# A fused attention and two-layer kernel: the attention's norms and layer one's low parts move from GpSimd to VectorE, with a new set of due times

## The chip, the cores and the metric

The kernel runs on one core of a Trainium2 chip. Its engines are TensorE (PE, with PEld for the loading of weights), VectorE (DVE), ScalarE (ACT), GpSimd (POOL) and SyncE (SP), which issues the DMAs here. The metric is the device time of one execution in microseconds (us). The kernel before takes 846.47 us, the median of three runs (845.16, 846.47, 847.29).

## The reference

An attention with local masks (a window of 32 rows in four heads, a dilated one in the other four) feeds two layers with weights. q, k and v are float32; the weight matrices arrive as float64 words and are decoded to float32 on the chip.

```python
scores = np.where(masks, q @ k.T / 8, -1e9)       # 4 batches, 8 heads, 576 rows, 64 wide
attn = exp(scores - max) / (sum + 1e-9)
x = (attn @ v)                                    # 2304 tokens x 512
h = ((x @ w1) * (x @ w2)) @ w3                    # 512 -> 1024 -> 1024
x = h @ w_out                                     # 1024 -> 512
h = x @ w_in                                      # 512 -> 2048
g = (a0 + a1*h + a2*h**2 + a3*h**3) / (1 + |b0|*|h| + |b1|*h**2 + 1e-6)
out = g @ w_out2                                  # 2048 -> 512
```

## The kernel before

Tokens stand along the free dimension, in five chunks of 480 (one of 384). Each value that enters a large matmul is kept as a high part (rounded to the matmul's format) and a low part (value minus high part), so that a product is made of three matmuls (`SPLIT`, L103).

The **first phase** (`phase1`, L589) does four things. It multiplies w3 by w_out once (`w3_mm`, L493), in plain float32, into eight tiles that are split into high and low (L504, L509). It runs the attention in 32 groups G of two heads and three row tiles of 96 (`att_qk` L375, `att_mask` L391, `att_exp` L408, `att_sums` L414, `att_norm` L420, `att_pt` L426, `att_pc` L433, `att_pv` L439). `att_high` and `att_low` (L480, L487) write x as high and low part into xs. For each chunk k, layer one (`l1`, L513) makes eight pairs of products of 12 matmuls each in the two banks `ab`; ScalarE copies the first (`l1_copy`), VectorE multiplies it with the second straight from its bank (`l1_mul`, L531), ScalarE casts the high part (`l1_high`, L536) and GpSimd subtracts for the low part (`l1_low`, L540). Layer two (`l2`, L543) follows in eight jobs of 12; its results leave their banks through ScalarE (L564) and VectorE (`x2l`, L569) and go to a DRAM tensor x2d. The fifth chunk's layer two is done in the second phase.

Weights arrive as 64-bit words in slabs of 512 KB (`load`, L243) and are decoded by a chain on ScalarE and VectorE: scale L257, shift L261, sign L265, low bits L280. With `by_act` a slab takes another route: ScalarE does one pass more (`top_bits`, L287) and VectorE only two (`ends` L292, `middle` L296). `BY_ACT3` is how many of the 24 slabs of w3 and w_out go by it. The slabs of w1 and w2 are split after that (L302, L306). The 32 slabs of the second phase's weights (moe2) are decoded one after the other through one slot, `w32`, and stored to a DRAM tensor wd (L310); the first four come back in `b_load` (L580) after the last of these stores.

**What sets the order.** Nothing of the first phase is in program order by hand. `Plan` (L114) holds each instruction group as a job with an engine, an estimated duration, what it follows, the buffers it takes and a due time. `dues` hands due times back along the dependences (`lead` shifts one; LEADS does so slab by slab), and `order` (L170) runs through time and gives each free engine the ready job that is due first. A job flagged `port`, and every POOL job, waits for the others so flagged. `tail` is the time from a job's end until another engine may start on it. The list sorted by start is what is issued, and each engine then works in that order, waiting in its queue. T (L613 to L617) holds nominal times of the main matmuls, with layer one and two stretched by PACE. The attention's due times hang on T, AHEAD, GAP and EARLY (L633 to L635), LEAD holds a group's start back, and B_FROM is where the due times of the moe2 stores begin (L809).

The **second phase** (`phase2`, L876) is a loop over 72 steps in program order: 12 matmuls (L906), the rational function on all of ScalarE, VectorE and GpSimd (L915 to L943), and 12 matmuls into the output (L956).

Of the kernel before, what the change touches and what calls it, by code (L numbers as in the profile page):

```python
# [10 lines left out]
F32 = mybir.dt.float32  # L11
# [4 lines left out]
ALU = mybir.AluOpType  # L16
# [10 lines left out]
CH = ((0, 480), (480, 480), (960, 384), (1344, 480), (1824, 480))  # L27
# [30 lines left out]
W3BANKS = (("acc", "ab"), ("acc", "ab"))  # L58


GAP0, GAP = 2.48, 9.89
LEAD = 83.96
AHEAD0, AHEAD = 10.57, 8.37
W3_AT = 8
PACE = 1.26

LEADS = (10.3, 12.3, 18.7, 24.0, 19.9, 5.3, 1.1, 21.6, 0.5, 9.0, -2.5, 3.0, -2.0, 35.8, -4.5, 15.1, -0.6, 1.0, -0.2, 3.4, -16.8, 2.7, -14.5, -8.7, -29.3, -24.1, -5.4, -5.8, -18.0, 1.2, -6.5, -5.3, -14.2, -16.4, -13.0, 2.4, -9.4, -18.5, -46.9, 13.0)
EARLY = (0.0, 0.6, 0.6, 0.5, 0.4, -2.9, -8.7, -2.1, 2.0, 3.3, -5.4, 10.3, -24.2, 19.9, 18.0, 2.9, 30.7, 24.0, 19.9, 23.2, 9.7, 2.9, -23.6, -53.8, -24.5, -67.9, -60.2, -3.4, -20.3, 1.3, 30.3, 41.5)
BY_ACT3 = 12
BY_ACT1, BY_ACT2 = 0, 16  # L70
B_FROM = 103.59


L2BANKS = (("acc", "ab"), ("acc", "sc"))
# [39 lines left out]
class Plan:  # L114
# [10 lines left out]
    def add(self, eng, work, fn, *args, after=(), new=(), use=(), due=None, port=False, tail=None,  # L125
            since=0.0, lead=0.0):


        if tail is None:
            tail = {"SP": 2.0, "PE": 0.2}.get(eng, 0.1)  # L130
        j = Job(len(self.jobs), eng, work, fn, args, [x for x in after if x is not None], new, due,
                port or eng == "POOL", tail, since, lead)
        for b in list(new) + list(use):
            b["users"].append(j)
        self.jobs.append(j)
        return j
# [83 lines left out]
class Kern:  # L220
# [199 lines left out]
    def att_norm(self, G, h):  # L420
        pr, sm = self.pr[G], self.sm[G]
        i = slice(3 * h, 3 * h + 3)
        self.nc.gpsimd.tensor_tensor(out=pr[:, i], in0=pr[:, i], op=ALU.mult,  # L423
                                     in1=sm[:, 2, i].unsqueeze(2).to_broadcast([QT, 3, P]))

    def att_pt(self, G, h):  # L426
# [110 lines left out]

    def l1_low(self, k, m):
        nt, w = CH[k][1], self.p2[k, m]
        self.nc.gpsimd.tensor_tensor(out=w[:, 1, 0:nt], in0=self.pp[k, m], in1=w[:, 0, 0:nt].bitcast(F32),  # L540
                                     op=ALU.subtract)

    def l2(self, k, h, i):  # L543
# [45 lines left out]
    def phase1(self):  # L589
# [20 lines left out]
        def act(k):  # L610
            return 0.08 + 0.00085 * CH[k][1]
# [9 lines left out]
        for ops in att_runs(2 * B * HP):  # L621
# [35 lines left out]
            for G, sc in qs:  # L657
                prb, smb, pTb = buf("pr"), buf("sm"), buf("pT")
                m0 = add("DVE", 0.64, self.att_mask, G, 0, after=[run], new=[prb, smb], use=sc[0:1])
                m1 = add("DVE", 0.64, self.att_mask, G, 1, after=[run, m0], use=[prb, smb, sc[1]])  # L660
                masked[G] = m1
                es = [add("ACT", 1.17, self.att_exp, G, h, after=[m], use=[prb, smb]) for h, m in enumerate((m0, m1))]
                su = add("DVE", 0.31, self.att_sums, G, after=es, use=[smb])
                no = [add("POOL", 0.79, self.att_norm, G, h, after=[su], use=[prb, smb]) for h in range(2)]
                pcs = []
                for h in range(2):
                    pb = buf(t_bank(G))
                    pt = add("PE", 0.25, self.att_pt, G, h, after=[no[h], done.get(G - 2)], new=[pb], use=[prb])
                    pts.setdefault(G, []).append(pt)
                    pcs.append(add("ACT", 0.31, self.att_pc, G, h, after=[pt] + pcs,  # L670
                                   new=[pTb] if h == 0 else [], use=[pb] + ([pTb] if h else [])))
                out[G] = pTb, pcs
# [88 lines left out]
        def l1_jobs(k, m):  # L761
            tb = [buf("t"), buf("t")]
            mm = []
            ready = [low[G] for b in range(B) if k in self.chunks(b) for G in range(b * 2 * HP, (b + 1) * 2 * HP)]
            for e in range(2):
                ab = buf("ab")
                mm.append((add("PE", mm12(k), self.l1, k, m, e, new=[ab], use=[xsb[k], w12b[2 * m + e]],
                               after=ready + [w12[2 * m + e]] + l1s[-1:], due=T["l1", k, m, e]), ab))
                l1s.append(mm[-1][0])
            d = T["l1", k, m, 1]  # L770
            c = add("ACT", act(k), self.l1_copy, k, m, after=[mm[0][0]], new=tb[0:1], use=[mm[0][1]], due=d)
            mu = add("DVE", act(k) + 0.09, self.l1_mul, k, m, after=[c, mm[1][0]], new=tb[1:2],
                     use=[tb[0], mm[1][1]], due=d + 2)
            pl, gbs = parts.setdefault(k, ([], []))
            gbs.append(buf("g"))
            hi = add("ACT", act(k) + 0.02, self.l1_high, k, m, after=[mu], new=gbs[-1:], use=[tb[1]], due=d + 5)
            pl.append(add("POOL", 0.08 + 0.0024 * CH[k][1], self.l1_low, k, m, after=[hi], use=[tb[1], gbs[-1]]))

        def l2_jobs(k):
            pl, gbs = parts[k]  # L780
# [346 lines left out]
```

## Time and profile before

| | us |
|---|---|
| median of three runs | 846.47 (845.16 to 847.29) |
| profiled execution | 844.74 |
| its span, first to last instruction | 842.9 |
| TensorE busy | 828.5 (98%) |
| VectorE busy | 581.2 (69%) |
| ScalarE busy | 539.4 (64%) |
| GpSimd busy | 330.5 (39%) |
| first matmul of the second phase (L906) | at 420.14 |

The profile is one execution, taken by the hardware profiler. Busy times are the union of an engine's instructions; a share over the whole span mixes two phases with different limits, so it is read by stages. "Idle before" is how long an engine stood before an instruction, and the releaser is the instruction that ended it. Starts are counted from the first instruction. L numbers are lines of the kernel.

### The profile page before, as it was taken

Reading aid. Unit: us, or ns where it says so; the run is one execution under the profiler, and the core shown is the slowest. Engines: PE = TensorE matmul, PEld = TensorE weight load, DVE = VectorE, ACT = ScalarE, POOL = GpSimd, SP = SyncE. Lnnn points to the kernel's source line nnn. Section 1 sums busy time; section 2 is a strip of 40 time slices with the busy share of each in tenths; the row PEclk is TensorE's granted clock in tenths of the full one; section 3 lists DMA queues with packets and bytes.
Section 4 is the critical chain, followed back from the end, with each engine's and each line's share of the span. In section 5 each row is a group of like instructions: output and inputs, shape, how many; then the busy total and the mean of one; then the engine's idle time right before and its main releaser. Section 6 shows DMA issues by size and latency. Waiting matters only on the chain.

```text
span 842.9 us, 12610 instructions
## 1 busy us (share of the span) xinstructions
PE 828.5 (98%) x4392; PEld 679.7 (81%) x4392; DVE 581.2 (69%) x1220; ACT 539.4 (64%) x1198; POOL 330.5 (39%) x289
## 2 busy tenths in 40 slices
PE   9999999999999989999999999999999999999998
PEld 6455788888889988888888788888888888888886
DVE  6899898555556644333327888788778777787775
ACT  6699885466456623312328877777777777786773
POOL 1123334133312411201215665565556556574442
PEclk9999999999999999999999999999999999999999
DMA  8988323554454234394151000010001000001112
GB/s 314 323 301 326 123 86 123 203 175 136 131 205 160 88 119 143 113 335 146 26 181 51 13 25 13 26 28 22 14 14 38 25 13 13 14 26 50 51 43 82
DMA packets 38271, 90.99 MB, mean 108 GB/s; under 512 B 4160, under 2 KB 9280, under 8 KB 38208
## 3 DMA queue, kind: packets, MB, share of 16 engines
q1 hardware_dynamic: 38208, 90.20, 31.7%
q8 instruction: 34, 0.56, 0.3%
q14 instruction: 29, 0.24, 0.1%
HBM read 69.60 MB, written 20.58 MB: 107 GB/s over the span
## 4 chain that ended last, share of the span: by engine, by line
PE 78%; DVE 8%; ACT 6%; DMA 5%; issue 2%; POOL 1%; SPq 0%; DVEq 0%; ACTq 0%; POOLq 0%
PE ab L519 21%; PE acc L956 11%; PE sc L956 11%; PE ab L906 10%; PE px L906 10%; PE acc L554 5%; DMA words<-moe_w 3%; PE sc L554 2%; PE ab L554 2%; ACT pr L411 2%; PE acc L445 1%; DMA words<-moe_w_out 1%; DVE dec L261 1%; PE sc L383 1%; DVE dec L265 1%
## 5 line engine op out<-in xcount | busy, mean ns | idle before, releaser
L519 PE MATMUL ab<-xs,w 128*128 128x480 f32 (+1 forms) x960 | 208.6, 374 | 4.1 <-DVE p L531 2.1
L519 PEld LDWEIGHTS ab<-xs,w 128*128 128x128 f32 x960 | 175.5, 188 | 28.8 <-DVE x2l L569 2.7
L917 POOL TENSOR_TENSOR y<-y,v 128x512 f32<-128x512 f32 x72 | 95.8, 1330 | 142.3 <-ACT y L916 142.1
L423 POOL TENSOR_TENSOR pr<-pr,sm 96x384 f32<-96x384 f32 x64 | 56.6, 907 | 170.9 <-DVE sm L418 98.0
L956 PE MATMUL acc<-w,gg 128*128 128x512 f32 x432 | 109.7, 391 | 1.5 <-ACT r L927 1.5
L956 PE MATMUL sc<-w,gg 128*128 128x512 f32 x432 | 109.3, 390 | 0.0
L540 POOL TENSOR_TENSOR pp<-p,pp 128x480 fp32r<-128x480 f32 (+1 forms) x40 | 50.1, 1256 | 141.9 <-ACT pp L536 141.9
L906 PE MATMUL ab<-XS,w 128*128 128x512 f32 (+1 forms) x480 | 105.4, 370 | 0.0
L906 PE MATMUL px<-XS,w 128*128 128x512 f32 (+1 forms) x480 | 105.3, 370 | 0.0
L943 POOL TENSOR_TENSOR gg<-t,gg 128x512 fp32r<-128x512 f32 x72 | 93.7, 1301 | 10.4 <-ACT gg L942 9.8
L906 PEld LDWEIGHTS px<-XS,w 128*128 128x128 f32 x480 | 83.8, 188 | 16.4
L906 PEld LDWEIGHTS ab<-XS,w 128*128 128x128 f32 x480 | 83.8, 188 | 16.4
L956 PEld LDWEIGHTS acc<-w,gg 128*128 128x128 f32 x432 | 80.7, 188 | 19.3 <-ACT r L927 1.9
L956 PEld LDWEIGHTS sc<-w,gg 128*128 128x128 f32 x432 | 80.8, 188 | 17.3
L411 ACT ACTIVATE pr<-pr,sm 96x128 f32<-96x128 f32 x192 | 74.4, 392 | 6.3 <-DVE sm L403 6.2
L257 ACT ACTIVATE dec<-words 128x512 f32<-128x512 f32 x72 | 48.0, 673 | 45.6 <-DMA words<-moe_w_in 21.3
L934 DVE SCALAR_TENSOR_TENSOR v<-y,cs,r 128x512 f32<-128x512 f32 x72 | 71.3, 991 | 0.0
L261 DVE TENSOR_SCALAR dec<-dec 128x512 int32<-128x512 int32 x44 | 28.8, 655 | 59.9 <-ACT dec L257 59.9
L926 ACT ACTIVATE r<-y,cs 128x512 f32<-128x512 f32 x72 | 52.3, 726 | 14.3 <-POOL y L917 14.1
L916 ACT ACTIVATE y<-v,cs 128x512 f32<-128x512 f32 x72 | 58.9, 817 | 2.5
L536 ACT CAST pp<-p 128x480 fp32r<-128x480 f32 (+1 forms) x40 | 23.1, 576 | 49.4 <-DVE p L531 49.3
L942 ACT CAST gg<-t 128x512 fp32r<-128x512 f32 x72 | 44.2, 614 | 14.2 <-DVE t L936 13.6
(96 smaller groups left out, 1295.1 us busy)
## 6 DMA issues: line engine op xcount, KB each, us to landing
words<-moe_w SPq DMA_DIRECT2D x32, 512.0 KB, 5.8
words<-moe_w_out SPq DMA_DIRECT2D x24, 512.0 KB, 4.4
words<-moe_w_in SPq DMA_DIRECT2D x16, 512.0 KB, 3.6
wd<-dec SPq DMA_DIRECT2D x32, 256.0 KB, 2.2
c<-wd SPq DMA_DIRECT2D x32, 256.0 KB, 2.7
vb<-v SPq DMA_DIRECT2D x16, 384.0 KB, 4.3
XS<-x2d SPq DMA_DIRECT2D x6, 1024.0 KB, 7.2
kT<-k SPq DMA_DIRECT2D x16, 304.0 KB, 4.2
```

The costliest lines, as they stand in the source:

```text
L411: self.nc.scalar.activation(out=pr[:, i], in_=pr[:, i], func=AF.Exp, scale=-1.0, bias=sm[:, 0, i:i + 1], accum_out=sm[:, 1, i:i + 1])
L423: self.nc.gpsimd.tensor_tensor(out=pr[:, i], in0=pr[:, i], op=ALU.mult, in1=sm[:, 2, i].unsqueeze(2).to_broadcast([QT, 3, P]))
L519: self.nc.tensor.matmul(t[:, 0:nt], w[:, s[0], c * P:(c + 1) * P], xs[:, s[1], c], start=n == 0, stop=n == 11)
L540: self.nc.gpsimd.tensor_tensor(out=w[:, 1, 0:nt], in0=self.pp[k, m], in1=w[:, 0, 0:nt].bitcast(F32), op=ALU.subtract)
L554: self.nc.tensor.matmul(self.l2_acc[k, n][:, 0:nt], self.W3o[m][0][:, a, n * P:(n + 1) * P], self.p2[k, m][:, c, 0:nt], start=m == 0 and ( ...
L906: nc.tensor.matmul(t[:, e * nt:(e + 1) * nt], w[:, s[0], c * P:(c + 1) * P], XS[blk][:, s[1], c], start=n == 0, stop=n == 11)
L916: nc.scalar.activation(out=w, in_=v, func=AF.Identity, scale=self.b1, bias=self.b0)
L917: nc.gpsimd.tensor_tensor(out=w, in0=w, in1=v, op=ALU.mult)
L926: nc.scalar.activation(out=r, in_=yy[i][1], func=AF.Ln, bias=self.c1)
L934: nc.vector.scalar_tensor_tensor(out=v, in0=w, scalar=self.c1, in1=r, op0=ALU.add, op1=ALU.mult)
L943: nc.gpsimd.tensor_tensor(out=t[:, 1], in0=u, in1=t[:, 0].bitcast(F32), op=ALU.subtract)
L956: nc.tensor.matmul(acc[g, blk][tk], t[:, s[0], j:j + P], w[:, s[1]], start=f + e == 0 and s == (0, 0), stop=f + e == FG - 1 and s == (1, 0))
```

## The change

Two functions issue on VectorE instead of GpSimd, `att_norm` (64 calls) and `l1_low` (40 calls), and their jobs in the plan move to VectorE with estimates of 0.48 us and `act(k) + 0.09`. All constants of the plan are replaced; BY_ACT3 goes from 12 to 21, B_FROM from 103.59 to 149.19, and the default `tail` becomes 0.27 for TensorE and 0.17 for the others. The instructions of the second phase are as before.

```diff
--- before.py
+++ after.py
@@ -58,17 +58,17 @@
 W3BANKS = (("acc", "ab"), ("acc", "ab"))
 
 
-GAP0, GAP = 2.48, 9.89
-LEAD = 83.96
-AHEAD0, AHEAD = 10.57, 8.37
+GAP0, GAP = 2.76, 10.61
+LEAD = 104.67
+AHEAD0, AHEAD = 18.65, 11.96
 W3_AT = 8
-PACE = 1.26
-
-LEADS = (10.3, 12.3, 18.7, 24.0, 19.9, 5.3, 1.1, 21.6, 0.5, 9.0, -2.5, 3.0, -2.0, 35.8, -4.5, 15.1, -0.6, 1.0, -0.2, 3.4, -16.8, 2.7, -14.5, -8.7, -29.3, -24.1, -5.4, -5.8, -18.0, 1.2, -6.5, -5.3, -14.2, -16.4, -13.0, 2.4, -9.4, -18.5, -46.9, 13.0)
-EARLY = (0.0, 0.6, 0.6, 0.5, 0.4, -2.9, -8.7, -2.1, 2.0, 3.3, -5.4, 10.3, -24.2, 19.9, 18.0, 2.9, 30.7, 24.0, 19.9, 23.2, 9.7, 2.9, -23.6, -53.8, -24.5, -67.9, -60.2, -3.4, -20.3, 1.3, 30.3, 41.5)
-BY_ACT3 = 12
+PACE = 1.34
+
+LEADS = (18.7, -11.8, -10.5, -0.6, -7.0, -7.1, -6.4, -0.0, -3.1, -13.2, -13.3, -1.9, 24.0, 46.2, 63.4, 50.6, 24.8, 5.1, 0.5, -4.7, 2.2, 10.1, 0.6, 16.9, -20.0, -11.2, -4.5, 5.6, 1.7, -4.0, 4.0, -1.1, -7.9, -5.3, 1.5, -21.3, -39.6, -55.7, -25.2, 57.4)
+EARLY = (1.1, -10.6, 3.3, -0.5, -9.6, -10.1, -15.1, -10.4, -29.7, -18.4, -23.1, -26.7, -36.5, -62.3, -44.5, -11.7, 11.4, 39.3, 44.0, 47.8, 16.0, 3.3, 8.5, -22.7, 7.1, 20.8, 2.0, -17.2, -6.8, -1.6, -60.0, 8.8)
+BY_ACT3 = 21
 BY_ACT1, BY_ACT2 = 0, 16
-B_FROM = 103.59
+B_FROM = 149.19
 
 
 L2BANKS = (("acc", "ab"), ("acc", "sc"))
@@ -127,7 +127,7 @@
 
 
         if tail is None:
-            tail = {"SP": 2.0, "PE": 0.2}.get(eng, 0.1)
+            tail = {"SP": 2.0, "PE": 0.27}.get(eng, 0.17)
         j = Job(len(self.jobs), eng, work, fn, args, [x for x in after if x is not None], new, due,
                 port or eng == "POOL", tail, since, lead)
         for b in list(new) + list(use):
@@ -420,7 +420,7 @@
     def att_norm(self, G, h):
         pr, sm = self.pr[G], self.sm[G]
         i = slice(3 * h, 3 * h + 3)
-        self.nc.gpsimd.tensor_tensor(out=pr[:, i], in0=pr[:, i], op=ALU.mult,
+        self.nc.vector.tensor_tensor(out=pr[:, i], in0=pr[:, i], op=ALU.mult,
                                      in1=sm[:, 2, i].unsqueeze(2).to_broadcast([QT, 3, P]))
 
     def att_pt(self, G, h):
@@ -537,7 +537,7 @@
 
     def l1_low(self, k, m):
         nt, w = CH[k][1], self.p2[k, m]
-        self.nc.gpsimd.tensor_tensor(out=w[:, 1, 0:nt], in0=self.pp[k, m], in1=w[:, 0, 0:nt].bitcast(F32),
+        self.nc.vector.tensor_tensor(out=w[:, 1, 0:nt], in0=self.pp[k, m], in1=w[:, 0, 0:nt].bitcast(F32),
                                      op=ALU.subtract)
 
     def l2(self, k, h, i):
@@ -661,7 +661,7 @@
                 masked[G] = m1
                 es = [add("ACT", 1.17, self.att_exp, G, h, after=[m], use=[prb, smb]) for h, m in enumerate((m0, m1))]
                 su = add("DVE", 0.31, self.att_sums, G, after=es, use=[smb])
-                no = [add("POOL", 0.79, self.att_norm, G, h, after=[su], use=[prb, smb]) for h in range(2)]
+                no = [add("DVE", 0.48, self.att_norm, G, h, after=[su], use=[prb, smb]) for h in range(2)]
                 pcs = []
                 for h in range(2):
                     pb = buf(t_bank(G))
@@ -774,7 +774,7 @@
             pl, gbs = parts.setdefault(k, ([], []))
             gbs.append(buf("g"))
             hi = add("ACT", act(k) + 0.02, self.l1_high, k, m, after=[mu], new=gbs[-1:], use=[tb[1]], due=d + 5)
-            pl.append(add("POOL", 0.08 + 0.0024 * CH[k][1], self.l1_low, k, m, after=[hi], use=[tb[1], gbs[-1]]))
+            pl.append(add("DVE", act(k) + 0.09, self.l1_low, k, m, after=[hi], use=[tb[1], gbs[-1]]))
 
         def l2_jobs(k):
             pl, gbs = parts[k]
```

## Rows read from the trace of the kernel before

**Rows 1.** The page: span, and each engine's busy us, share, instructions.

```profile
span 842.9 us, 12610 instructions
PE 828.5 (98%) x4392; PEld 679.7 (81%) x4392; DVE 581.2 (69%) x1220; ACT 539.4 (64%) x1198; POOL 330.5 (39%) x289
```

**Rows 2.** Windows: length; busy us of PE, PEld, DVE, ACT, POOL; clock; DMA.

```profile
29.20:83.20 54.00, 53.15 (x321) 28.45 (x321) 52.12 (x202) 48.04 (x174) 15.92 (x16) 1.00 0.89 320
83.20:92.20 9.00, 7.38 (x86) 6.18 (x85) 8.37 (x22) 8.74 (x28) 3.50 (x4) 0.81 0.76 265
92.20:117.00 24.80, 24.80 (x158) 21.27 (x157) 22.75 (x53) 21.21 (x59) 8.11 (x7) 1.00 0.27 82
117.00:134.00 17.00, 15.52 (x77) 12.63 (x76) 16.03 (x41) 11.23 (x38) 6.93 (x7) 1.00 0.21 71
292.00:315.40 23.40, 20.60 (x141) 19.77 (x139) 12.15 (x19) 7.22 (x21) 4.88 (x6) 1.00 0.31 102
315.40:420.10 104.70, 104.65 (x480) 90.11 (x481) 36.68 (x54) 28.73 (x50) 18.57 (x15) 1.00 0.46 154
420.10:843.00 422.90, 417.49 (x1921) 346.42 (x1920) 318.61 (x443) 302.83 (x469) 222.43 (x171) 1.00 0.12 37
```

**Rows 3.** Timeline of TensorE: start, us, instruction, idle before it and its releaser.

```profile
85.16 0.47 PE L430 MATMUL sc<-ident,pr 96*128 96x96 f32 x3 [0.32 <-POOL pr L423]
86.71 0.44 PE L430 MATMUL px<-ident,pr 96*128 96x96 f32 x3 [1.09 <-DVE xs L489]
```

**Rows 4.** Windows, one microsecond after those stalls (columns as in rows 2).

```profile
89.00:90.00 1.00, 1.00 (x12) 0.78 (x10) 1.00 (x2) 1.00 (x3) 0.00 (x0) 0.50 0.21 66
```

**Rows 5.** Timeline of TensorE, the later stalls that carry a releaser.

```profile
133.40 2.86 PE L519 MATMUL ab<-xs,w 128*128 128x480 f32 x12 [0.97 <-DVE p L531]
291.11 2.35 PE L519 MATMUL ab<-xs,w 128*128 128x384 f32 x12 [0.81 <-DVE p L531]
305.81 1.21 PE L445 MATMUL acc<-pT,vb 128*64 128x96 f32 x24 [0.86 <-DVE x2l L569]
315.42 42.47 PE L519 MATMUL ab<-xs,w 128*128 128x480 f32 x192 [1.96 <-DVE x2l L569]
```

**Rows 6.** Timeline of VectorE and GpSimd ahead of the stall at 133.40.

```profile
124.51 3.23 DVE L261 TENSOR_SCALAR dec<-dec 128x512 int32<-128x512 int32 x1
126.24 2.58 POOL L540 TENSOR_TENSOR pp<-p,pp 128x480 fp32r<-128x480 f32 x2
```

**Rows 7.** Groups by line and shape: count, busy us, mean ns, idle before.

```profile
L423 POOL TENSOR_TENSOR pr<-pr,sm 96x384 f32<-96x384 f32 x64 | 56.6, 907 | 170.9 <-DVE sm L418 98.0 <-ACT pr L411 63.5 <-ACT pT L436 9.0
L261 DVE TENSOR_SCALAR dec<-dec 128x512 int32<-128x512 int32 x44 | 28.8, 655 | 59.9 <-ACT dec L257 59.9
L265 DVE SCALAR_TENSOR_TENSOR dec<-words,dec 128x512 int32<-128x512 int32 x44 | 38.0, 863 | 1.3
L531 DVE TENSOR_TENSOR p<-a_sb,ab 128x480 f32<-128x480 f32 x28 | 18.2, 650 | 26.2 <-PE ab L519 15.0 <-issue 7.9 <-PE px L430 3.3
L531 DVE TENSOR_TENSOR p<-a_sb,ab 128x384 f32<-128x384 f32 x8 | 4.4, 551 | 3.1 <-PE sc L430 1.8 <-PE ab L519 1.0 <-ACT pr L411 0.3
```

**Rows 8.** Lines L261 and L265: ns min/median/max, first and last start.

```profile
L261 DVE TENSOR_SCALAR dec<-dec x44: 381/427/3231, 24.0 to 393.0; 128x512 int32<-128x512 int32 x44
L265 DVE SCALAR_TENSOR_TENSOR dec<-words,dec x44: 678/693/2376, 24.4 to 393.4; 128x512 int32<-128x512 int32 x44
```

**Rows 9.** Timeline of ScalarE: first of twelve exponentials, and the cast behind them.

```profile
117.11 0.40 ACT L411 ACTIVATE pr<-pr,sm 96x128 f32<-96x128 f32 x1
121.74 0.58 ACT L536 CAST pp<-p 128x480 fp32r<-128x480 f32 x1
```

**Rows 10.** Timeline of SP's DMA issues: moe2 slabs, and the split's first loads.

```profile
149.45 0.37 SPq L243 DMA_DIRECT2D words<-moe_w_in  x1
388.77 0.37 SPq L243 DMA_DIRECT2D words<-moe_w_out  x1
396.10 1.92 SPq L580 DMA_DIRECT2D c<-wd  x2
```


## Prediction

> **What bounds the kernel now.** I read the page first: TensorE is busy in 828.5 of 842.9 us [rows 1], so no rebalancing of the other engines can win more than TensorE's gaps, 14.4 us, plus what it loses at a lower clock. The busy times by stage say where those gaps are [rows 2]. The second phase, 420.1 to 843, leaves 422.90 - 417.49 = 5.41 us, and none of its lines is edited. The stretch 315.4 to 420.1, in which no attention is left, leaves 0.05. What remains lies in five places: 29.2 to 83.2 leaves 0.85; 83.2 to 92.2, where layer one waits for the first batch's attention, 1.62; 117 to 134, 1.48; a stall at 291.11 of 0.81 [rows 5]; and 292 to 315.4, 2.80. Together 7.56 us.
>
> One loss is not idle time: in 83.2 to 92.2 the mean granted clock is 0.81 [rows 2], and between 89 and 90 it is 0.50, the lower of the two levels (1.2 and 2.4 GHz), right after TensorE had stood for 0.32 and 1.09 us [rows 3, 4]. That costs 9.0 x (1 - 0.81) = 1.7 us if the engine would have been busy. So 7.56 + 1.71 = **9.3 us** is all that a new order of the first phase can win.
>
> Next I asked what releases TensorE in those places, and what had held the releaser. The stall before 133.40 (0.97) waits for the product p of VectorE [rows 5]. VectorE was late because one integer shift, L261, took 3.23 us from 124.51 [rows 6]; the median of 44 such shifts is 0.427 us, the shortest 0.381 [rows 8]. GpSimd was at work beside it, from 126.24 on two low parts [rows 6]. So these two engines hold each other up: L261 has a mean of 0.655 against a median of 0.427, L265 0.863 against 0.693 [rows 7, 8]. Over 44 of each that is 10.0 + 7.5 = 17.5 us of VectorE time. The products L531, which read a PSUM bank, take 0.650 on the mean in the same stretches [rows 7].
>
> **The change part by part.** (1) The norms. 64 instructions of 96x384 leave GpSimd, at 0.907 us each [rows 7], and join VectorE. The trace has no such operation there; by row length the nearest are L531 at 384 elements, 0.551, and at 480, 0.650 [rows 7]. The planner's own figure, 0.48, is the low end, 0.55 the high one. So 64 x 0.48 to 0.55 = 31 to 35 us. (2) The low parts: 32 of 480 and 8 of 384 elements. The planner's 0.58 and 0.50 against 0.65 and 0.55 give 23 to 25 us. Nothing excludes slightly less than the planner says, since successive instructions overlap at their ends, but not below zero: each is a whole pass. (3) What VectorE gets back: at least the 17.5 us above, since no GpSimd instruction stands beside it after the constants. (4) BY_ACT3 from 12 to 21: nine slabs are decoded by the other route, on VectorE 0.70 + 0.62 for 0.45 + 0.72 + 0.62 by the planner's figures, so 9 x 0.47 = 4.2 us less on VectorE and 9 x 0.59 = 5.3 us more on ScalarE. Net, VectorE gains 54 to 60 less 22, some 32 to 38 us over 420. Its busy time there is 581.2 - 318.6 = 262.6 us [rows 1, 2]; it would become 295 to 301, 70 to 72%. That is hidden behind TensorE wherever no single stretch fills up.
>
> So stretch by stretch. In 29.2 to 92.2 VectorE is busy 52.12 + 8.37 of 63 us, 2.5 idle; 16 + 4 GpSimd instructions are there, all norms as layer one has not begun [rows 2]. They bring 9.6 to 11.0; back come 4.2 from the slabs and, at the mean rate of the lock over 420 us (an estimate), 17.5 x 63 / 420 = 2.6. Net 2.8 to 4.2 on 2.5 of room: 0.3 to 1.7 us too much, unless the new order puts off some of the decoding of w1 and w2. Layer one takes two of those sixteen slabs every 5.2 us, so the later ones need not be ready by then; I take nothing as lost, with 1.7 as the bound. ScalarE is busy 48.04 + 8.74 there [rows 2], 6.2 idle, and takes the 5.3: full, but not over.
>
> In 92.2 to 134, 7 + 7 GpSimd instructions [rows 2] bring about 8 us to VectorE, while the one slow decode at 124.5 alone gives back 2.8 in its shift [rows 6, 8], and B_FROM (103.59 to 149.19) gives the moe2 slabs' stores later due times. Each such slab is a 512 KB load and a 256 KB store on SP's queue, one ScalarE and three VectorE instructions. All of these fall behind layer one, the attention's loads and the stores of x2 in priority. The moved work goes toward 315.4 to 420, where VectorE has 104.7 - 36.7 = 68 us idle [rows 2]. Cost there nothing, as long as the last store comes in time (rival four).
>
> (5) A new wait: l1_low must wait on VectorE for ScalarE's cast of the same product. On GpSimd that wait held up nobody. Now the next masks, products, sums and decodes stand behind it. The norm adds none, as the sums just ahead of it wait for the same exponentials. (6) LEADS, EARLY, LEAD, GAP, AHEAD, PACE and the tails (0.1 to 0.17, TensorE 0.2 to 0.27) change the list's order and add no instruction. Their effect can't be read from the trace: at most the 9.3 us above back, and below nothing if the new order meets waits of its own.
>
> **The sum.** Of the 9.3 us I give back those that rows tie to GpSimd. The stall before 133.40: 0.97, whole, as the shift was 2.8 us late and the stall is shorter. The 0.32 before 85.16, which waits for a norm on GpSimd [rows 3]: 0.32 whole, as the norm shortens by 0.36 or more. The 1.09 before 86.71 waits for VectorE's low part of xs [rows 3]; with VectorE full there I take half, 0.55, bounds 0 and 1.09. The slow clock follows those two; the 1.7 us are lost whole or not at all, and I take 60%, 1.0. The x2l waits, 0.86 and 1.96 [rows 5]: the moe2 decode ahead of x2l in VectorE's queue began late; a third, 0.95, bounds 0 and 2.8. The stall at 291.11 has no GpSimd work just before it: nothing. Total 3.8 us. Of the profiled execution, 844.74 us (842.9 span and 1.8 around it), that leaves 840.9; its time is 1.7 below the median of the three runs, 846.47, so against the median **842.7 us**.
>
> **The rivals.** *One, every stall goes:* the re-timed list fits better now that VectorE's times are steady. 846.5 - 9.3 = 837.2 at best, some 838 to 839.5. For it: the stalls are few and each has a late releaser. Against it: three of five places were not GpSimd's. *Two, the gain goes into new stalls:* the order is new in every place, in-order queues give 1 to 2 us stalls at the chunks' boundaries, and VectorE is fuller by 32 to 38 us: 844 to 849. The change not doing what it says belongs here, if VectorE's slow decodes had another cause than GpSimd; the steady medians speak against that.
>
> *Three, slower: the new wait of l1_low.* ScalarE runs a group's exponentials in a row; twelve of them in a row stand in its queue from 117.11, and the cast comes only at 121.74, 4.6 us later [rows 9]. If a cast lands behind such a row, VectorE stands for it. The product that frees the bank has the length of one TensorE group, 12 x 218 ns = 2.6 us (104.65 us over 480 matmuls [rows 2]), less its own 0.65: 1.96. So each case costs up to 4.6 - 2.0 = 2.7 us. From three full cases on the gain of 3.8 is gone; with four, 4 x 2.7 - 3.8 = +7, 853. For it: 40 such waits, in a queue that is 92% busy (22.75 of 24.80) [rows 2] while layer one begins. Against it: the list counts ScalarE's end into the order, and of TensorE's stalls before only those at 133.40 and 291.11 were waits for the product [rows 5].
>
> *Four, slower: the moe2 slabs end too late.* The last is loaded at 388.77 and the split's first loads follow at 396.10 [rows 10], 24 us before the second phase's first matmul at 420.1. Five slabs were loaded by 149.45, and from there 27 intervals to 388.77 took 8.9 us each [rows 10]. If four fewer are done by then and none is caught up, the end moves 4 x 8.9 = 35 us, 11.6 past the slack: 846.5 + 11.6 - 3.8 = 854. Against it: the locked shifts stretched just this chain.
>
> *Five, slower: VectorE full before layer one.* Rows first: 60.49 of 63 us busy in 29.2 to 92.2 [rows 2], and up to 11.0 us more of norms. With no payback at all layer one would start 11.0 - 2.5 = 8.5 us later; with the other 2.3 us of gain, 852.7. The Trainium skill (Perfetto Trace Analysis, section Optimizing Scalar/DVE Operations) advises the opposite of this change: where VectorE is saturated, work may be given to ScalarE or even GpSimd. The same section warns that VectorE and GpSimd share a port, so that a trade between them might not help, and the 3.23 us shift agrees with that.
>
> **How the numbers follow.** Forecast (840 to 844): 0.46. Rival one: 0.10. Two: 0.25. Three: 0.10. Four: 0.04. Five: 0.05. About 0.3%, 2.5 us, is what a measurement of this kernel can tell from no change. Faster than 843.9: 0.45 of the forecast and rival one, 0.55. Within 843.9 to 849.0: 0.26, rival two and the forecast's edge. Slower: 0.19, three to five. The range 838.0 to 850.5 leaves out the lowest end of rival one and most of three to five.
>
> **What would show it.** Right: L261 and L265 at their medians in mean as well; GpSimd idle from the constants to the second phase; VectorE near 297 us busy in the first phase; no 0.5 clock near layer one's start, or a shorter one; the first L906 matmul at 416 to 417. Wrong: VectorE idle before L540 for ScalarE's cast with TensorE waiting for p behind it (three); TensorE waiting on the split of c at the end (four); layer one starting after 93 (five); or shifts that stay slow with GpSimd idle.

## The result, and the profile after

The changed kernel takes 836.16 us, the median of four runs (835.93 to 836.82), against 845.85 for the kernel before with one more run beside it: a ratio of 0.9885, 95% interval 0.9867 to 0.9902. That is 9.7 us less, where 3.8 were forecast, and it lies below the range of 838.0 to 850.5.

The page of the kernel after (span, engines, and the shares of the chain that ended last):

```profile
span 834.2 us, 12542 instructions
PE 825.7 (99%) x4392; PEld 678.5 (81%) x4392; DVE 600.6 (72%) x1315; ACT 543.8 (65%) x1207; POOL 224.2 (27%) x185
PE 94%; DVE 2%; ACT 2%; issue 2%; POOL 0%; POOLq 0%; DVEq 0%
```

The span falls by 8.7 us, from 842.9 [rows 1], and TensorE's idle time from 14.4 to 8.5 us. VectorE is busy 19.4 us longer over the span, GpSimd 106 us less. The chain that ended last is now TensorE's to 94%; in the kernel before it was 78%.

Its busy times by stage, with the columns of rows 2:

```profile
0.00:15.10 15.10, 12.12 (x69) 9.30 (x70) 8.22 (x35) 10.05 (x25) 2.98 (x15) 0.89 0.86 323
15.10:86.80 71.70, 71.68 (x365) 36.29 (x363) 67.22 (x190) 64.32 (x186) 0.00 (x0) 1.00 0.87 304
86.80:134.00 47.20, 47.20 (x344) 40.49 (x345) 44.09 (x166) 40.36 (x140) 0.00 (x0) 1.00 0.33 101
134.00:300.00 166.00, 166.00 (x1178) 149.19 (x1178) 112.06 (x402) 93.66 (x336) 0.00 (x0) 1.00 0.48 151
307.00:411.40 104.40, 104.40 (x481) 90.22 (x482) 44.86 (x73) 29.79 (x51) 0.00 (x0) 1.00 0.48 166
411.40:834.30 422.90, 417.44 (x1921) 346.58 (x1919) 320.47 (x446) 303.29 (x470) 221.27 (x170) 1.00 0.12 37
```

From 15.1 to 411.4 TensorE stands for some 0.14 us altogether. Layer one starts at 86.80 instead of 92.20 [rows 2], the second phase at 411.38 instead of 420.14. The second phase is as long as before, 422.9 us, with 5.5 us of gaps for 5.4, so all of the gain lies in the first phase: 8.76 us between the two profiles.

To split these 8.76 at layer one's start, the work on either side has to be the same, and it is not: the kernel before had done ten groups' transposes and values and twelve groups' scores by then, the one after eight and ten. Two groups cost TensorE some 3.6 us, as its timeline after shows: four transposes 97.38 to 98.32, two groups' values and scores 101.11 to 103.73. The first two rows belong to the start.

```profile
9.51 0.46 PE L383 MATMUL sc<-kT,qT 64*96 64x128 f32 x2 [0.92 <-DVE sm L403]
11.54 3.67 PE L499 MATMUL acc<-x 128*128 128x512 f32 x4 [0.51 <-DVE x L296]
...
97.38 0.41 PE L430 MATMUL sc<-ident,pr 96*128 96x96 f32 x3
98.32 2.86 PE L519 MATMUL ab<-xs,w 128*128 128x480 f32 x12
101.11 1.21 PE L445 MATMUL acc<-pT,vb 128*64 128x96 f32 x24
103.73 1.58 PE L519 MATMUL ab<-xs,w 128*128 128x480 f32 x6
```

So ahead of layer one the change gains 5.40 - 3.6 = 1.8 us, and from there to the second phase, 324.58 us instead of 327.94, it gains 3.36 + 3.6 = 7.0. The 1.8 are not clear of chance: two single profiles of the same early list differ by up to 2.4 us there (last section).

The start itself is not better. Two groups' scores go ahead of the first product of w3 and w_out, which begins at 11.54 (before: 8.39), and after the gaps of 0.92 and 0.51 us TensorE runs at the lower clock, in one microsecond of the window view (columns as in rows 2):

```profile
12.00:13.00 1.00, 1.00 (x2) 0.34 (x1) 1.00 (x8) 1.00 (x7) 0.00 (x0) 0.50 1.02 387
```

The profile's clock record has 3.41 us at 0.50 there, from 11.69, where the kernel before had 3.41 us from 88.47 [rows 4]. The slow stretch was not won back, it moved.

VectorE's groups after, from 0 to 400 us (to set beside rows 7):

```profile
L423 DVE TENSOR_TENSOR pr<-pr,sm 96x384 f32<-96x384 f32 x64 | 33.0, 551 | 1.0
L265 DVE SCALAR_TENSOR_TENSOR dec<-words,dec 128x512 int32<-128x512 int32 x35 | 24.2, 692 | 1.1
L540 DVE TENSOR_TENSOR pp<-p,pp 128x480 fp32r<-128x480 f32 x29 | 18.8, 655 | 7.5 <-ACT pp L536 7.1
L261 DVE TENSOR_SCALAR dec<-dec 128x512 int32<-128x512 int32 x35 | 14.8, 424 | 36.1 <-ACT dec L257 36.1
```

L261 has come from 0.655 to 0.424 us and L265 from 0.863 to 0.692, their old medians [rows 8]. The norm takes 0.551 and the low part 0.655, the high ends of the two ranges.

### The profile page after: what moved, and what is told of

Read it like the earlier page. It is cut to its first block, busy times and chain, and to the rows that moved or that the text cites. A ratio compares the mean times of both kernels' runs of the same rounds, so it can differ in the third digit from the quotient of the medians.

```text
span 834.2 us, 12542 instructions
## 1 busy us (share of the span) xinstructions
PE 825.7 (99%) x4392; PEld 678.5 (81%) x4392; DVE 600.6 (72%) x1315; ACT 543.8 (65%) x1207; POOL 224.2 (27%) x185
## 4 chain that ended last, share of the span: by engine, by line
PE 94%; DVE 2%; ACT 2%; issue 2%; POOL 0%; POOLq 0%; DVEq 0%
PE ab L519 24%; PE acc L956 11%; PE sc L956 11%; PE ab L906 11%; PE px L906 11%; PE acc L554 6%; PE acc L499 4%; PE ab L554 3%; PE ab L499 3%; PE sc L383 2%; PE acc L445 2%; PE sc L554 1%; PE px L430 1%; PE px L383 1%; PE px L339 1%
## 5 line engine op out<-in xcount | busy, mean ns | idle before, releaser
L519 PE MATMUL ab<-xs,w 128*128 128x480 f32 (+1 forms) x960 | 205.9, 373 | 0.1
L531 DVE TENSOR_TENSOR p<-a_sb,ab 128x480 f32<-128x480 f32 (+1 forms) x40 | 25.3, 633 | 40.7 <-PE ab L519 31.3
L554 PE MATMUL acc<-pp,w 128*128 128x480 f32 (+1 forms) x240 | 51.2, 371 | 0.0
L554 PEld LDWEIGHTS acc<-pp,w 128*128 128x128 f32 x240 | 44.2, 188 | 5.5
```

Source lines behind the costliest of these rows:

```text
L519: self.nc.tensor.matmul(t[:, 0:nt], w[:, s[0], c * P:(c + 1) * P], xs[:, s[1], c], start=n == 0, stop=n == 11)
L554: self.nc.tensor.matmul(self.l2_acc[k, n][:, 0:nt], self.W3o[m][0][:, a, n * P:(n + 1) * P], self.p2[k, m][:, c, 0:nt], start=m == 0 and ( ...
```

## The experiments

Two theories at the start: **A**, GpSimd and VectorE held each other up, and with that gone TensorE's stalls go; **B**, the new due times did it. The first three runs give either part alone, twice for one of them. Each ratio is to the kernel before on the same chip. Line numbers in rows are those of the kernel shown: where an experiment adds lines, its later lines stand one to six further down (the norm L423 is L424 in one of them).

### The old list, the operations on VectorE

```diff
 # the kernel before, constants and planned jobs (POOL) unchanged
-        self.nc.gpsimd.tensor_tensor(out=pr[:, i], in0=pr[:, i], op=ALU.mult,
+        self.nc.vector.tensor_tensor(out=pr[:, i], in0=pr[:, i], op=ALU.mult,
...
-        self.nc.gpsimd.tensor_tensor(out=w[:, 1, 0:nt], in0=self.pp[k, m], ...
+        self.nc.vector.tensor_tensor(out=w[:, 1, 0:nt], in0=self.pp[k, m], ...
```

> The list of the kernel before, planned for GpSimd, but the norms and the low parts issued on VectorE at their old places. Theory A: the 0.97 us stall before layer one's seventh product, the 0.32 us wait for a norm and the slow clock before layer one go, 840 to 843 us. Theory B: the stalls move but stay, 845 to 850 us; VectorE may stand for ScalarE's cast before L540, as the old list gave no room for that wait.

Measured: 840.64 us, ratio 0.9941 (0.9924 to 0.9958), 4.9 us faster. Busy times by stage (columns as in rows 2), ahead of layer one and after it:

```profile
29.20:86.00 56.80, 54.22 (x320) 28.45 (x320) 55.83 (x218) 49.30 (x178) 0.00 (x0) 1.00 0.85 308
95.20:416.50 321.30, 321.18 (x1984) 282.80 (x1981) 199.36 (x611) 163.46 (x503) 0.00 (x0) 1.00 0.44 146
```

Layer one starts at 95.25, three microseconds *later* than before. From there to the second phase it takes 321.28 us instead of 327.94, and TensorE stands for 0.1 us in all of it. Both kernels issue the same matmuls in the same order, so they can be laid beside each other matmul by matmul: at the start of layer one this kernel is 3.05 us behind, and it wins 2.0 from 120 to 133.4 (times of the kernel before), 1.0 at 291.11, 0.9 at 305.81 and 1.8 at 315.42, the places of [rows 5], and 0.9 in smaller steps. Every stall that stood behind layer one is gone, with the order of the list unchanged: theory A is right there, with 6.7 us. TensorE's two longest waits that are left (us in total, times, longest), beside the wait at the very start and one in the second phase:

```profile
PE px L430 <- DVE xs L489: 3.5, 3, 1.6
PE px L430 <- DVE sm L403: 0.8, 1, 0.8
```

All of it stands before layer one, where VectorE is busy 55.83 of 56.8 us. Ahead of layer one the expectation failed: the stalls there stayed, and so did the slow clock, with 3.41 us at 0.50 from 90.90 by the clock record.

The stall at 291.11 [rows 5] shows how far a held-up decode reaches. In the kernel before, VectorE, GpSimd and SP stood so some ten microseconds ahead of it:

```profile
277.25 2.16 DVE L265 SCALAR_TENSOR_TENSOR dec<-words,dec 128x512 int32<-128x512 int32 x1
279.44 1.39 DVE L280 SCALAR_TENSOR_TENSOR dec<-words,dec 128x512 int32<-128x512 int32 x1
285.55 0.43 DVE L261 TENSOR_SCALAR dec<-dec 128x512 int32<-128x512 int32 x1 [3.98 <-ACT dec L257]
278.82 1.47 POOL L540 TENSOR_TENSOR pp<-p,pp 128x384 fp32r<-128x384 f32 x1
281.29 0.37 SPq L243 DMA_DIRECT2D words<-moe_w_in  x1
```

L265 took 2.16 us and L280 1.39, beside four norms and two low parts on GpSimd (274.5 to 280.3). The decode ended at 280.84, 2.0 us later than in this run; the store and the next load of this one-slot chain came that much later, the next decode fell at 285.55 to 287.43, and there the masks of two groups, whose scores were ready by then, stood behind it; the product p stood behind the masks. With nothing on GpSimd the last line of the same decode is, in this run:

```profile
278.19 0.69 DVE L280 SCALAR_TENSOR_TENSOR dec<-words,dec 128x512 int32<-128x512 int32 x1
```

and the stall does not occur. The two stalls behind x2l came the same way. The next decode in the kernel before had a shift of 2.40 us, beside two norms and a low part:

```profile
294.04 2.40 DVE L261 TENSOR_SCALAR dec<-dec 128x512 int32<-128x512 int32 x1
302.71 0.67 ACT L257 ACTIVATE dec<-words 128x512 f32<-128x512 f32 x1 [5.65 <-DMA words<-moe_w_in]
```

Its store went out at 298.61 (in this run at 295.86), so ScalarE's scale of the next slab waited longer for its load. ScalarE's casts of layer two's results (L564), at 303.27, stood behind that scale, and VectorE's x2l behind the decode that followed, to 305.20.

### The new list, the operations on GpSimd

```diff
 # the changed kernel, constants and planned jobs (DVE) unchanged
-        self.nc.vector.tensor_tensor(out=pr[:, i], in0=pr[:, i], op=ALU.mult,
+        self.nc.gpsimd.tensor_tensor(out=pr[:, i], in0=pr[:, i], op=ALU.mult,
...
-        self.nc.vector.tensor_tensor(out=w[:, 1, 0:nt], in0=self.pp[k, m], ...
+        self.nc.gpsimd.tensor_tensor(out=w[:, 1, 0:nt], in0=self.pp[k, m], ...
```

> The list of the changed kernel, planned as if for VectorE, but the norms and the low parts issued on GpSimd (the other part alone). Theory A: L261 and L265 are slow again and TensorE stalls again, 844 to 849 us. Theory B: the order itself keeps TensorE fed, 836 to 839 us.

Measured: 842.1 us, ratio 0.995 (0.9934 to 0.9967): between the two theories, 3.5 us faster than before and 5.9 slower than with VectorE. Layer one starts at 90.72 and the stretch from there takes 327.40 us (86.80 and 324.58 on VectorE). TensorE's waits that came back:

```profile
PE px L430 <- POOL pr L423: 1.8, 2, 1.0
PE px L430 <- ACT pT L436: 1.4, 2, 1.0
PE ab L519 <- DVE x2l L569: 0.8, 1, 0.8
```

So with the medians beside the kernel before of their own groups (845.6 and 845.85), the engine alone is worth 4.9 us, the list alone 3.5, both 9.7. They nearly add: the 1.3 us left over are less than the width of one of these intervals, 2.8 us.

### The operations on VectorE, planned anew with the old constants

```diff
 # the kernel before, both functions on nc.vector, and
-                no = [add("POOL", 0.79, self.att_norm, ...
+                no = [add("DVE", 0.48, self.att_norm, ...
...
-            pl.append(add("POOL", 0.08 + 0.0024 * CH[k][1], self.l1_low, ...
+            pl.append(add("DVE", act(k) + 0.09, self.l1_low, ...
```

> The norms and the low parts on VectorE with their new estimates, all constants of the plan as before (one part of the change alone; the list is planned anew). Theory A, the stalls of TensorE came from GpSimd and VectorE holding each other up: the stalls behind the product p and x2l go, some 4 to 6 us faster than before, 840 to 842 us, with L261 at a mean of 0.43 us. Theory B, the gain is in the new due times: within 2 us of before or slower, 844 to 850, with stalls in new places although L261 is at 0.43.

Measured: 850.48 us, ratio 1.0052 (1.0034 to 1.007), 4.9 us slower. L261 is at 0.422 in the mean, so VectorE is free of GpSimd, and yet layer one starts at 96.66. TensorE's longest waits:

```profile
PE px L430 <- DVE pr L423: 3.8, 3, 2.7
PE sc L430 <- ACT pr L411: 2.5, 1, 2.5
```

The old constants fit the old plan only. The same instructions on the same engines take 840.6 us in the old list and 850.5 in the one that the planner makes of them.

### One constant back at a time

```diff
-BY_ACT3 = 21
+BY_ACT3 = 12
```

> The changed kernel with BY_ACT3 back at 12, the list planned anew: nine slabs give VectorE 0.43 us more each, 3.9 us, and ScalarE two passes of 0.6 less in all nine, ahead of layer one, where VectorE is busy 67.2 of 71.7 us. If the new list's gain ahead of layer one (4.7 us against the old list, both with the operations on VectorE) comes from this: layer one starts 3 to 4 us later, near 90.5, 839 to 841 us. If it comes from the order: 836 to 837.5 us.

Measured: 845.78 us, as the kernel before (ratio 1.0003, 0.999 to 1.0017). That is worse than either expectation. TensorE's waits:

```profile
37.63 0.46 PE L383 MATMUL sc<-kT,qT 64*96 64x128 f32 x2 [1.22 <-DVE sm L403]
40.30 3.78 PE L499 MATMUL acc<-x 128*128 128x512 f32 x4 [0.78 <-DVE x L296]
93.24 2.02 PE L519 MATMUL ab<-xs,w 128*128 128x480 f32 x8 [1.14 <-DVE w L509]
```

Layer one starts 6.4 us later, at 93.24. The decode on VectorE is heavier, as meant, but the list is also another one: at 37 to 40 the scores of a group wait for banks that a late mask holds, and the first product after it for a slab. By the clock record TensorE then runs 6.83 us at 0.50, from 39.40.

```diff
-B_FROM = 149.19
+B_FROM = 103.59
```

> The changed kernel with B_FROM back at 103.59, the list planned anew: the moe2 slabs are due 45 us earlier and compete with layer one's first chunk for VectorE, ScalarE and SP. If that was what the later due time avoided: layer one as now at 86.8, some 1 to 3 us of stalls in 87 to 150 behind the product p, 837 to 839.5 us. If the slabs only fill idle time: 836 to 836.8 us.

Measured: 852.23 us, ratio 1.0091 (1.0061 to 1.0121), 16 us slower than the changed kernel and outside both expectations. One wait is the largest part of it:

```profile
130.75 0.82 PE L383 MATMUL px<-kT,qT 64*96 64x128 f32 x12
138.24 0.71 PE L430 MATMUL sc<-ident,pr 96*128 96x96 f32 x3 [6.66 <-DVE sm L416]
```

Here the list puts a group's transposes right behind its scores, with no product of layer one between, so that TensorE stands for the whole way through masks, exponentials, sums and norm, 6.66 us. The clock record has 10.24 us at 0.50 there, from 133.90, inside that stall, to 144.14, so that TensorE worked 5.7 us at the lower clock after it. So neither run measures its constant by itself: each made the planner lay out another list. What they show is that the constants hold only together, and how much one bad place costs.

### Work on GpSimd whose results nobody reads

Theory A leaves open *how* GpSimd costs time: by holding up VectorE, or because the transposes and layer two wait for its longer norm and low part. These runs give the changed kernel extra GpSimd work with no reader; it can only hold up VectorE, or keep a buffer longer.

```diff
 # in att_norm, after the norm on VectorE
+        for t in range(3):
+            self.nc.gpsimd.tensor_tensor(out=self.scr, in0=self.masks[:, t], op=ALU.mult,
+                                         in1=sm[:, 2, 3 * h + t:3 * h + t + 1].to_broadcast([QT, P]))
...
 # in l1_low, after the low part on VectorE
+        self.nc.gpsimd.tensor_tensor(out=self.pp[k, m], in0=self.pp[k, m], in1=w[:, 0, 0:nt].bitcast(F32),
+                                     op=ALU.subtract)
```

> The changed kernel, and beside each norm and each low part on VectorE a second pass on GpSimd over the same lengths that nobody needs: three products of 96x128 into a scratch tile, and a subtraction that overwrites the product p after its last reader. So GpSimd works where it did in the kernel before, but no chain runs through it, save that buffers come free a little later. If VectorE's slow decodes come from GpSimd's work beside them, and these made the stalls: L261 at a mean over 0.55 us, TensorE's stalls back, 839 to 843 us. If the longer norm on the path to the transposes made them: L261 may be slow, but 836 to 838 us.

Measured: 848.98 us, ratio 1.0037 (1.0023 to 1.0051): 12.8 us slower than the changed kernel, by work whose result goes nowhere. L261 rose to 0.495 up to 400 us (0.518 with the last decodes), less than expected, but L265 to 0.790, and the stalls are back:

```profile
L265 DVE SCALAR_TENSOR_TENSOR dec<-words,dec 128x512 int32<-128x512 int32 x33 | 26.1, 790 | 1.0
L261 DVE TENSOR_SCALAR dec<-dec 128x512 int32<-128x512 int32 x33 | 16.3, 495 | 43.2 <-ACT dec L257 43.1
L427 POOL TENSOR_TENSOR scr<-masks,sm 96x128 bf16<-96x128 f32 x192 | 132.5, 690 | 133.3 <-DVE sm L419 119.6
```

```profile
PE ab L523 <- DVE p L535: 2.6, 2, 1.9
PE acc L503 <- DVE x L296: 2.3, 4, 0.8
PE sc L384 <- DVE sm L404: 1.9, 4, 0.9
PE px L434 <- DVE pr L424: 1.5, 3, 0.9
```

The dose is larger than in the kernel before: GpSimd is busy 178 us in the first 411.4, against 106. And it is not all hold-up: by the profile ScalarE stood 3.0 us in two waits, and VectorE 1.2 us in one, for buffers that the extra work kept. Two smaller doses set each operation beside its shadow.

```diff
-self.nc.vector   # att_norm
+self.nc.gpsimd
```

> The changed kernel with the norms alone back on GpSimd, the list as it is. Both together cost 842.1 - 836.2 = 5.9 us, of which 3.9 stood ahead of layer one, where there are norms alone. So if the parts add up: 840 to 841.5 us, layer one starting near 90.7.

Measured: 841.14 us (ratio 0.9947, 0.9932 to 0.9962); layer one at 89.82, 327.25 us from there.

```diff
 # in att_norm: the three products above, cut to two; nothing in l1_low
+        for t in range(2):
```

> The changed kernel with two unneeded products of 96x128 on GpSimd after each norm, some 0.9 to 1.3 us of GpSimd per norm (the norm itself takes 0.9 to 1.0 there); nothing for the low parts. With the norms themselves on GpSimd layer one started at 89.8 and the stretch after it took 327.3 us. If holding up VectorE is the cause: layer one at 89 to 91, 327 to 329 us after it, 841 to 845 us. If it was the transposes' wait for GpSimd's longer norm: 86.8 to 88 and 324.6 to 326 us.

Measured: 839.43 us (0.9919, 0.9902 to 0.9935); layer one at 88.86, 326.05 us from there. Here it is the norm on VectorE itself that is slowed, from 0.551 to 0.631:

```profile
L424 DVE TENSOR_TENSOR pr<-pr,sm 96x384 f32<-96x384 f32 x64 | 38.1, 631 | 1.0
```

```diff
-self.nc.vector   # l1_low
+self.nc.gpsimd
```

> The changed kernel with layer one's low parts alone back on GpSimd, the list as it is. Layer one starts at 86.8 as in the changed kernel; 836.2 to 838.5 us. If the low parts hold up VectorE as much as the norms, 838 to 839.

Measured: 839.24 us (0.9928, 0.991 to 0.9945); layer one at 88.62, 326.32 us from there.

```diff
 # in l1_low: the second subtraction above; nothing in att_norm
```

> The changed kernel with a second, unneeded subtraction on GpSimd after each low part (it overwrites the product p after its last reader); no second pass for the norms. GpSimd is idle ahead of layer one. To be read is the stretch from layer one's start to the second phase, 324.6 us in the changed kernel and 326.3 with the low parts themselves on GpSimd. If holding up VectorE is what costs there: 326 to 327.5. If it was layer two's wait for GpSimd's longer low part: 324.6 to 325.

Measured: 838.61 us (0.99, 0.9883 to 0.9918); layer one at 89.23, 326.22 us from there, L261 at 0.511:

```profile
L261 DVE TENSOR_SCALAR dec<-dec 128x512 int32<-128x512 int32 x35 | 17.9, 511 | 42.5 <-ACT dec L257 42.2
```

Read the stretch from layer one to the second phase, 324.58 us in the changed kernel. The low parts on GpSimd add 1.7 us there and their shadow 1.6; the norms add 2.7 and their shadow, though it keeps GpSimd busier (97 us against 62), 1.5. In the norms' shadow no engine's wait behind the constants is put down to GpSimd, so there holding up VectorE is the whole cost. In the low parts' shadow ScalarE stood once for a buffer, 1.6 us at 201.52, and no matmul came later by it. So holding up VectorE is by itself enough for what the low parts cost, and for about half of what the norms cost. How the cost of the operations themselves divides is not shown, because the places differ. Laid beside the changed kernel matmul by matmul, the run with the norms on GpSimd falls behind at 98, 112, 126, 208 and 247 (times of the changed kernel), each time at a group's transposes, by 0.1 to 0.9 us, which fits the longer way through the norm; its shadow falls behind at 166, 177, 194 and 247. Ahead of layer one the single profiles cannot tell: the two kernels with nothing new on GpSimd there, those of the low part, still started layer one 1.8 and 2.4 us late (see the last section), and the profile of the low parts' shadow is the slowest of its five executions (span 838.3 us, the others 835.3 to 836.8).

The Trainium skill (SBUF — State Buffer, section Who interferes with whom) describes an exclusive lock on a port pair that both engines use, so that the one that comes second waits the other's whole instruction out. The shadows agree with it: no data pass from GpSimd to another engine, and the norm goes from 0.551 to 0.631 us and the shift from 0.424 to 0.511.

### The old list, with the first ten groups' norms left on GpSimd

```diff
 # the old list with both on VectorE, except
-        self.nc.vector.tensor_tensor(out=pr[:, i], in0=pr[:, i], op=ALU.mult,
+        eng = self.nc.gpsimd if G < 10 else self.nc.vector
+        eng.tensor_tensor(out=pr[:, i], in0=pr[:, i], op=ALU.mult,
```

> The list of the kernel before with both operations on VectorE, except the norms of the first ten groups, which stay on GpSimd. With all on VectorE this list started layer one at 95.25 (before: 92.20) and took 321.3 us from there (before: 327.9). If the late start came from VectorE being full: layer one at 92 to 93, 321 to 322 us after it, 837 to 838.5 us. If it came from something else: layer one at 95, 840.6 us.

Measured: 838.44 us, ratio 0.9918 (0.9898 to 0.9938). Layer one starts at 91.75, 3.5 us earlier than with all norms on VectorE (2.2 in the medians), and takes 320.95 us from there:

```profile
29.20:86.00 56.80, 55.35 (x348) 29.79 (x344) 55.17 (x209) 51.51 (x187) 18.69 (x20) 1.00 0.90 321
91.75:412.70 320.95, 320.83 (x1983) 282.72 (x1982) 199.12 (x607) 163.34 (x502) 0.00 (x0) 1.00 0.44 146
```

VectorE had worked 84.1 us by layer one's start with all norms on it and 80.1 in this run, four less, and layer one follows. So the late start with all norms on VectorE was VectorE's. The old list alone, with the work shared so, comes within 2.3 us of the changed kernel.

### The slow clock at the start

```diff
 # in att_qk, after the matmuls
+        if G < 2:
+            t = self.bank("px")
+            for i in range(5 - G):
+                self.nc.tensor.matmul(t[:, 0:P], self.ident, self.ident, start=True, stop=True)
```

> The changed kernel with 5 and 4 small matmuls more on TensorE, behind the first and the second group's scores, where it stands between 8.6 and 11.5 us; results of these are not used. If the 3.4 us at half clock from 11.7 cost what the rows say (half of them, 1.7 us, TensorE being full from there to layer one): no 0.5 clock after 5 us, layer one starts at 85.1 instead of 86.8, 834.5 us. If the start of layer one is set by VectorE or by the weights' loads instead: layer one at 86.8 and 836 us.

Measured: 837.26 us, ratio 0.99 (0.9882 to 0.9918), no faster than the changed kernel. The clock stays up, and yet:

```profile
9.13 1.38 PE L389 MATMUL px<-ident 128*128 128x128 f32 x10
11.58 1.16 PE L389 MATMUL px<-ident 128*128 128x128 f32 x8
12.57 1.88 PE L503 MATMUL acc<-x 128*128 128x512 f32 x4
87.05 10.74 PE L523 MATMUL ab<-xs,w 128*128 128x480 f32 x48 [0.38 <-DVE w L513]
```

The first product starts a microsecond later, at 12.57, at full speed (0.6 us of it because the scores start at 8.30 instead of 7.68, as the clock rose later in this profile), and layer one at 87.05, after a wait of 0.38 us for VectorE's low part of w3 times w_out. TensorE's 1.7 us at the lower clock were not on the path: VectorE ends that stretch, and TensorE only reaches it a little earlier or later. Nor is the slow stretch at 11.7 in every execution of this list: the profiles of the new list on GpSimd, of the low parts on GpSimd and of their shadow have none, and their layer one starts later, not earlier. No version here beats the changed kernel.

## Why the prediction was wrong

- **What bounds the kernel.** Right: the second phase did not move, and the first phase won no more than TensorE had lost. The bound of 9.3 us, "all that a new order of the first phase can win", was a little low as a sum of gaps. A stall costs more than its idle row, because the end of the last matmul before it is modelled too late: at 315.42 the idle is 1.96 [rows 5], but the last of the matmuls before it, 173 ns apart, starts at 313.12, so 2.1 were lost. With the old list and VectorE, 6.7 us went behind layer one where the rows had shown 5.1 of idle.
- **Costs of the moved work.** Right, at the high ends: 0.551 and 0.655 us, and the decodes at their medians. VectorE is busy 280 us of the first 411, against 262 of the same stretch before. The forecast of 295 to 301 was too high because the payback was more than the 17.5 us of two lines: other lines without an operand in PSUM had been slow too, as L416 (0.286 us before, 0.164 after) and L306 (0.822, 0.684), by some 13 us with L280, L292 and L296.
- **The term that failed most: the new list, its due times priced at nothing** for want of a row. With the operations on VectorE, the new list (due times and BY_ACT3 together) is worth 4.5 us (840.6 to 836.2), on GpSimd 3.5. The gain lies ahead of layer one. In the old list VectorE is full there and starts layer one at 95.25; the new list has it work 75.4 us by then instead of 84.1, as it does two groups fewer and decodes nine slabs by the lighter route, and TensorE stands for nothing from 15.1 on. Set on the same work, layer one comes at 86.80 + 3.6 = 90.4 instead of 95.25. Which constant does it is not settled, as each one changed alone gave another list.
- **The stalls behind layer one, under-sized.** I gave back 0.97 and a third of the x2l waits, 1.9 us in all; all of it went, 6.7 us with the old list. One step that failed is "the stall at 291.11 has no GpSimd work just before it: nothing". It was ten microseconds before, and the one-slot chain of the moe2 slabs carried it on. The other is the third of the x2l waits: the reason given there, a late moe2 decode, was right, and with it went all of them, 2.8 us. A releaser's delay must be followed back to its own releaser until an instruction is found that took longer than its median.
- **The stretch ahead of layer one, over-sized.** I gave back 1.9 us there (0.32, 0.55 and the slow clock's 1.0). With the old list the operations on VectorE cost 3.1 us there instead in the profiles, and 1.8 by the medians (6.7 - 4.9). Rival five, VectorE full, is real in the old list. My net of 0.3 to 1.7 us too much on VectorE had 4.2 us of BY_ACT3 in it; without them, as in the old list, the same sum gives 4.5 to 5.9, so it was too high. In the changed kernel rival five did not show: layer one starts at 86.80, not after 93. So the engine's part came out at 4.9 where I had 3.8, near only by luck, from two errors of opposite sign.
- **The slow clock.** It left layer one's start and stands at 11.7 in this profile, and taking it away won nothing (the run with small matmuls). What it had cost at layer one's start no run shows by itself; the old list on VectorE kept it there.
- **The other rivals.** Rival one, every stall goes, is what happened; I gave it 0.10 and put its time at 838 to 839.5, against 836.2. Rival two did not show in the changed kernel, whose TensorE stands for 0.14 us from 15.1 on; the lists planned from mixed constants (850.5, 845.8 and 852.2 us) are what it describes. Rival three did not decide: VectorE stands for ScalarE's cast before L540 in 14 waits up to 411 us, 8.3 us in all and 0.7 at most, and TensorE waits for none of them. Rival four did not show either: the second phase starts with no gap.
- **The advice against it.** The Trainium skill (Perfetto Trace Analysis, section Optimizing Scalar/DVE Operations) would give work of a full VectorE to GpSimd. Ahead of layer one the old list agrees, with 3.5 us in the mixed run (2.2 in the medians). Behind it VectorE is not full (199 of 321 us), so the advice does not reach there, and taking the work back from GpSimd won 6.7 us.

## What to carry to other kernels

Work on GpSimd is not free for VectorE, even where nobody waits for it: compare the mean of VectorE's longest lines with their medians, and where they part, move GpSimd's work over in those stretches where VectorE has room, and weigh it where VectorE is full. There the old list gained 2.2 us by leaving ten groups' norms on GpSimd; a list planned for VectorE with some norms left on GpSimd was not tried, and with all 64 norms there the changed kernel lost 5.0. A list made by a planner from tuned constants is one object: judge an edit by issuing it in the old list and in the new one, and do not read a constant's worth from changing it alone. When several waits of the critical engine hang on one in-order queue, look first for one cause that feeds them all: here three slow decodes stood behind four stalls.

## What the runs showed of the hardware

- TensorE's clock rises from the lower level in the first microseconds at a moment that differs from one execution to the next, from 4.2 to 7.5 us after the start in these fourteen profiles, with the same forty warming matmuls in all of them. These start 0.213 us apart before that moment and 0.112 after it; the window view has no entry for the time before it and shows 1.00. Two kernels whose lists up to layer one are the changed kernel's, without GpSimd work there, had the late rise: those with the low parts on GpSimd and with their shadow. VectorE's masks and the decode behind them, at 10.0 in the changed kernel, were 1.1 and 1.3 us late in them, and layer one started at 88.62 and 89.23 instead of 86.80.
- The clock is not all of that delay. In the second of them VectorE was only 0.3 us late at 46, and at 46.75 it was 2.3 (times of the changed kernel): ScalarE stood for the load of a weight slab, and VectorE 1.86 us behind it. In the first the same two waits were 1.24 and 0.73 us; in the changed kernel neither engine stood there. The row is the second one's. Why that slab landed later is not shown. In any case, differences of up to some 2.5 us ahead of layer one between two single profiles show nothing here.

```profile
48.31 0.67 ACT L287 ACTIVATE words<-words 128x512 int32<-128x512 uint8 x1 [2.37 <-DMA words<-moe_w]
```

- Small stalls of TensorE leave no idle row. In the run with the norms on GpSimd the way from layer one to the second phase grew by 2.7 us, and TensorE's idle time there by 0.85 (0.12 to 0.97); the rest came in small steps that only the matmul-by-matmul comparison shows.
- A VectorE instruction can be held up through more than one GpSimd instruction: the shift of 3.23 us [rows 6], 124.51 to 127.74, stood beside the end of one norm, two whole norms and one whole low part, and ended 0.3 us into the next low part.
- The products L531 with one operand in PSUM kept 0.650 us [rows 7] whatever GpSimd did: 0.652 without its work, 0.648 to 0.653 in the runs with it; the lines that slowed read and write SBUF alone.
